# Attention and a mixture of experts in one kernel: the gate computed in each expert slot, and the order of early loads and weight splits

## The chip, the cores and the metric

The kernel runs on one core of a Trainium2 chip. Its engines each run their own queue of instructions in order: TensorE (PE in the rows; its weight loads are PEld), VectorE (DVE), ScalarE (ACT), GpSimd (POOL), and SyncE (SP), whose queue here issues most of the DMA transfers. The metric is the time of one execution on the device in microseconds; the time before is the median of three runs.

## What is computed

```python
# attention over 32 memory slots; B, H, S, D, M = 8, 8, 576, 64, 32
a = softmax(phi, axis=seq)
k_m = einsum('bhsm,bhsd->bhmd', a, k); v_m = einsum('bhsm,bhsd->bhmd', a, v)
attn = softmax(q @ k_m.T / sqrt(D)); x = (attn @ v_m)   # as (4608 tokens, 512)
# mixture of 8 experts, one for each token
logits = x @ w_gate
e_idx = argmax(logits, axis=1)
gate_w = softmax(logits)[arange(N), e_idx]
eom = 1 / (1 + exp(-(x @ w_output_gate)))
for e in range(8):
    mask = e_idx == e
    out[mask] = gate_w[mask, None] * eom[mask, e, None] * (relu(x[mask] @ w1[e]) @ w2[e])
```

## The kernel before

**Attention.** The eight batches are worked in four pairs. For each pair `memory(bp)` takes phi through an exp (`soften`), transposes it, and multiplies it with nine chunks of k and v (`sums`, L778; chunks 0 to 7 are tiles kvt, chunk 8 is kv) into k_m and v_m; `turn_kv` (L804 on TensorE, L809 and L810 on ScalarE) makes kT. The 20 turns of `attention()`, five to a pair, each take a piece of q through scores (L869), shift, exp (L889), divide, transpose and values (L916, emptied by ScalarE in L918), and store rows of x to the DRAM table xs (L1055, L1059). A row of xs is four groups of 144 numbers: 128 of x, and 16 that are that group's share of the logits of w_gate and w_output_gate.

**Order.** `ORDER` lists the steps of a turn; at each step but w, f and G the generator yields, and what was deferred (`LATE`, `hold`) comes nearer. `MEM` and `MEM0` list the steps of `memory`. Loads are issued from `loads()`, a generator that `lod.step()` moves: `NLD` steps at the start, then one in each `sums(c)` with c < 8. All issues of SP stand in one queue in the order of the program.

**Ranking.** After the fifth turn of a pair `rank(bp)` picks each token's expert, counts, and places tokens in lists (`route_early`, `route_late`, `table`). It also computes the gate of the pair's tokens (w2_, w3_, zs, gd, gt) and writes it over the 16 columns behind the first 128 of each row in xs (`gates_out`, L1008 and L1011).

**Slots.** 36 slots of three, two or one block of 128 tokens of one expert are in `order`; 14 of them run here. `gather` reads a slot's rows of xs by indirect DMA into xg, `turn_x` turns them into xh and xl (high and low parts of fp32), `Stream.split` makes high and low parts of a piece of weights (ScalarE L587, VectorE L602; eight pieces to a slot), `several` does the matmuls (L1309 or L1304 and L1305, then L1346) and `finish_y` scales by the gate and scatters. The first five slots are whole (x is transposed by TensorE, L1140); the later ones are quartered (four gathers of 144 numbers to a block, transposed by VectorE). The first slot opens in turn 17 of attention; the rest of attention and of the ranking is stepped from `hook()` inside the slots. Two pieces of weights are split in turn 16, at the two places w in ORDER; f flushes the VectorE half.

The core of it, as far as the change needs it:

```python
ORDER = ["R4", "X", "S", "G", "R0", "m", "w", "D", "G", "M", "w", "B", "f", "V0", "R1", "R1", "V1", "M", "m", "f", "W", "C"]
...
                elif w == "w":
                    if t == START - 1:
                        stream.split(2, False)
                    continue
```

Of the kernel before, what the change touches and what calls it, by code (L numbers as in the profile page):

```python
# [9 lines left out]
F32 = mybir.dt.float32  # L10
# [8 lines left out]
P = 128  # L19
# [3 lines left out]
NCH = 9  # L23
# [15 lines left out]
ORDER = ["R4", "X", "S", "G", "R0", "m", "w", "D", "G", "M", "w", "B", "f", "V0", "R1", "R1", "V1", "M", "m", "f", "W", "C"]  # L39
# [9 lines left out]
NLD = 3  # L49
# [22 lines left out]
def attention_moe(tc, phiT, kv, qT, wgo, wall, out):  # L72
# [3 lines left out]
    with contextlib.ExitStack() as ctx:  # L76
# [138 lines left out]
        def table(nm, q, nch, nblk):  # L215
# [18 lines left out]
            yield from hold(LATE["pe"])  # L234
# [498 lines left out]
        def memory(bp):  # L733
# [33 lines left out]
            def sums(c):  # L767
# [17 lines left out]
                if c < 8:  # L785
                    lod.step()
                elif b and bp + 1 < NBP:
                    load_kv(bp + 1, 8)
# [143 lines left out]
        def rank(bp, lg):  # L932

            t0 = bp * 2 * S
            lt = lg[:, :, 0:E]
            lo = lg[:, :, E:2 * E]
# [4 lines left out]
            w2_ = rt.tile(b3, F32, name="w2_")  # L941
            w3_ = rt.tile(b3, F32, name="w3_")
            pm = rt.tile([P, NCH], F32, name="pm")
            zs = rt.tile([P, NCH], F32, name="zs")
            gd = rt.tile([P, NCH], F32, name="gd")
# [4 lines left out]
            gt = rt.tile([P, NCH, XQ - P], F32, name="gt")  # L950
# [6 lines left out]
            G.tensor_tensor(w2_[:], lt, lmb, ALU.subtract)  # L957
# [8 lines left out]
            V.tensor_tensor(w3_[:], oh, lo, ALU.mult)  # L966
            A.activation(w2_[:], w2_[:], AF.Exp)
# [5 lines left out]
            V.tensor_reduce(zs[:], w3_[:], axis=AX.X, op=ALU.add)  # L973
            yield

            def rest():
# [10 lines left out]
                V.tensor_reduce(gd[:], w2_[:], axis=AX.X, op=ALU.add)  # L987
                A.activation(zs[:], zs[:], AF.Exp, scale=-1.0)
# [4 lines left out]
                V.tensor_scalar(gd[:], gd[:], 1e-9, None, ALU.add)  # L993
# [3 lines left out]
                V.tensor_scalar(zs[:], zs[:], 1.0, None, ALU.add)  # L997
# [3 lines left out]
                V.tensor_tensor(gd[:], gd[:], zs[:], ALU.mult)  # L1001
                yield
                V.tensor_copy(row[:], ri[:])  # L1003
                V.reciprocal(gd[:], gd[:])
                yield
                V.tensor_copy(gt[:], gd[:].unsqueeze(2).to_broadcast([P, NCH, XQ - P]))
                def gates_out(b):
                    nc.sync.dma_start(  # L1008
                        xs[t0 + b * S:t0 + b * S + 512, P:XQ].rearrange("(c p) d -> p c d", p=P),
                        gt[:, 4 * b:4 * b + 4])  # L1010
                    nc.sync.dma_start(xs[t0 + b * S + 512:t0 + b * S + 576, P:XQ], gt[64 * b:64 * b + 64, 8])  # L1011
# [4 lines left out]
                if bp == 1 and "open" not in env:  # L1016
                    kept.extend(functools.partial(gates_out, b) for b in range(2))
                    singly.extend(functools.partial(one_hot, c) for c in range(NCH))
                else:
                    for b in range(2):  # L1020
                        gates_out(b)
# [82 lines left out]
        def turn_x(z, c):  # L1104
# [4 lines left out]
            if c == 0:  # L1109
                z["x"] = (mo.tile([P, 4, 3 * P], F32R, name="xh"),  # L1110
                          None if nb == 2 else mo.tile([P, 4, 3 * P], F32R, name="xl"))
                if z["quart"]:
                    z["xt"] = {}
                    z["g"] = env["xt"].tile([P, 3], F32, name="gx")
                    for b in range(4):
                        k = nb - (nb == 2 and b > 1)
                        A.copy(z["g"][32 * b:32 * b + 32, 0:k], xg[0:32, 0:k, XQ * b + P])
            xh, xl = z["x"]
            if z["quart"]:
# [9 lines left out]
                if nb == 2:  # L1129
                    pt = z["xt"].pop(c)[:, 0:192]  # L1130
                    A.copy(xh[:, c, 0:192], pt)
                    V.tensor_tensor(xh[:, c, 192:384], pt, xh[:, c, 0:192].bitcast(F32), ALU.subtract)
                    return
                pt = z["xt"].pop(c)[:, 0:n]
# [8 lines left out]
            V.tensor_tensor(xl[:, c, 0:n], pt, xh[:, c, 0:n].bitcast(F32), ALU.subtract)  # L1143

# [126 lines left out]
        def finish_y(z, k, py):  # L1271
            y = mo.tile([P, DM], F32, name="y", bufs=2)
            n = P
            if (z["nb"], k) == (2, 1):

                n = 64
                ya = env["xt"].tile([64, DM], F32, name="ya", bufs=1)
                A.copy(ya[:], py[64:128])
                V.tensor_tensor(ya[:], py[0:64], ya[:], ALU.add)
                py = ya[:]  # L1280
            A.activation(y[0:n], py[0:n], AF.Copy, scale=z["g"][0:n, k:k + 1] if z["quart"] else z["xg"][:, k, P:P + 1])  # L1281
# [4 lines left out]
        def several(i, st, nxt, hook):  # L1286


            z = order[i]
            nb, x, h = z["nb"], z["x"], []  # L1290
            n_ = nb * P
            for u in range(4):
# [36 lines left out]
                hook()  # L1329
            py = [bank([DM], "ps") for _ in range(nb)]  # L1330
# [26 lines left out]
        def single(i, st, nxt):  # L1357
# [15 lines left out]
            for u in range(4):  # L1373
# [13 lines left out]
                if u < 3:  # L1387
                    st.done(PUMP[1])
            for c in range(5):
                nxt(c)  # L1390
# [36 lines left out]
        def run(st):  # L1427
# [95 lines left out]
```

## Time and profile before

| what | value |
|---|---|
| median of three runs | 551.75 us (550.49 to 555.39) |
| the profiled execution | 547.47 us |
| its span, first to last instruction | 545.8 us |
| TensorE busy | 505.4 us (93%) |
| VectorE busy | 352.2 us (65%) |
| ScalarE busy | 287.5 us (53%) |
| GpSimd busy | 238.7 us (44%) |
| mean granted clock of TensorE | 0.973 of 2.4 GHz |
| DMA | 123.54 MB, mean 226 GB/s |

The rows come from the one profiled execution, whose own time lies below all three runs; a sum of its durations stands against 547.47 us. A busy TensorE means that a matmul is in flight, and the ends of matmuls are modelled; where two follow each other, the distance of their starts is what counts. The time in front of a bracket such as [2.60 <-DMA qt<-qT] is how long the engine was idle before the row, and what ended it.

### The profile page before, as it was taken

How to read it: one execution, taken by the hardware profiler on the slowest of the kernel's cores; microseconds unless marked ns; L12 is line 12 of the kernel's file. 1: busy time of each engine (PE TensorE's matmuls, PEld its weight loads, DVE VectorE, ACT ScalarE, POOL GpSimd, SP SyncE). 2: the span in 40 equal slices, each digit the busy share in tenths (PEclk: the TensorE clock that was granted, in tenths of full speed). 3: DMA queues.
4: the chain of work that ended last, by engine and by line, in shares of the span. 5: the costliest groups of instructions: out<-in, count | busy, mean ns of one | idle time of the engine just before them, and what ended most of it. 6: DMA issues, size and time to landing. Idle time of an engine off the chain costs nothing. (4 is left out here: it accounts for less than half of the span.)

```text
span 545.8 us, 10567 instructions
## 1 busy us (share of the span) xinstructions
PE 505.4 (93%) x3850; PEld 437.8 (80%) x3850; DVE 352.2 (65%) x783; ACT 287.5 (53%) x536; POOL 238.7 (44%) x254
## 2 busy tenths in 40 slices
PE   3768688799999999999999999999999999999993
PEld 2445466598789898898998989898999899898982
DVE  4275999868865559978446546953886297639310
ACT  3465567644454365453444546853776376548310
POOL 2152568673525044320476553564447353710101
PEclk9978989989999999999999999999999999999998
DMA  8999999798767658754566574865686477743101
GB/s 282 413 410 413 410 344 368 275 367 281 205 211 237 202 199 291 223 156 131 155 189 202 178 235 134 266 217 186 212 251 198 164 249 238 236 133 98 30 20 44
DMA packets 42062, 123.54 MB, mean 226 GB/s; under 512 B 10320, under 2 KB 10384, under 8 KB 41616
## 3 DMA queue, kind: packets, MB, share of 16 engines
q1 hardware_dynamic: 35200, 102.71, 57.3%
q0 software_dynamic: 6800, 20.06, 10.4%
q8 instruction: 32, 0.52, 0.4%
q14 instruction: 30, 0.25, 0.1%
HBM read 102.40 MB, written 20.35 MB: 225 GB/s over the span
## 5 line engine op out<-in xcount | busy, mean ns | idle before, releaser
L1346 PE MATMUL bps<-whl,hh 128*128 128x512 f32 x640 | 192.3, 393 | 0.0
L1309 PE MATMUL bps<-xh,whl 128*128 128x384 f32 x640 | 166.7, 337 | 0.0
L602 DVE TENSOR_TENSOR whl<-w,whl 128x1024 fp32r<-128x1024 f32 x112 | 136.3, 1222 | 9.6 <-ACT whl L587 9.6
L1346 PEld LDWEIGHTS bps<-whl,hh 128*128 128x128 f32 x640 | 119.9, 188 | 24.5 <-issue 0.2
L587 ACT CAST whl<-w 128x1024 fp32r<-128x1024 f32 x112 | 116.1, 1044 | 13.8 <-PE bps L1346 13.7
L1309 PEld LDWEIGHTS bps<-xh,whl 128*128 128x128 f32 x640 | 116.5, 189 | 1.2 <-issue 0.6
L542 POOL DMA_INDIRECT xg<-xs,idx_ql x84 | 99.0, 1178 | 25.6 <-issue 23.5
L1309 PE MATMUL bps<-xl,whl 128*128 128x384 f32 x320 | 107.4, 336 | 0.0
L1346 PE MATMUL bps<-whl,hl 128*128 128x512 f32 x240 | 93.7, 390 | 0.0
L1314 DVE SCALAR_TENSOR_TENSOR hl<-bps,hh 128x384 fp32r<-128x384 f32 x80 | 44.0, 554 | 64.4 <-ACT hh L1313 64.4
L1313 ACT ACTIVATE hh<-bps 128x384 fp32r<-128x384 f32 x80 | 38.9, 492 | 77.0 <-PE bps L1309 73.9
L1282 POOL DMA_INDIRECT out<-y,idx_ol x23 | 25.8, 1121 | 109.7 <-ACT y L1281 54.1
L1309 PEld LDWEIGHTS bps<-xl,whl 128*128 128x128 f32 x320 | 60.5, 189 | 0.4
L1346 PEld LDWEIGHTS bps<-whl,hl 128*128 128x128 f32 x240 | 45.1, 188 | 8.5
L885 POOL TENSOR_TENSOR ea<-ea,mx 128x512 f32<-128x512 f32 (+1 forms) x20 | 19.3, 963 | 47.3 <-DVE mx L883 42.1
L1304 PE MATMUL bps<-xh,whl 128*128 128x384 f32 x128 | 37.7, 338 | 0.0
L1305 PE MATMUL bps<-xh,whl 128*128 128x256 f32 x128 | 35.7, 279 | 0.0
L1281 ACT ACTIVATE y<-bps,gx 128x512 f32<-128x512 f32 x19 | 13.1, 687 | 40.1 <-PE bps L1346 33.4
L1014 POOL TENSOR_SCALAR Aw<-iota_row,row 128x128 bf16<-128x128 bf16 x36 | 29.1, 824 | 8.4 <-DVE row L1003 8.3
L1282 POOL DMA_INDIRECT out<-y,idx_ob x9 | 10.8, 1200 | 46.6 <-ACT y L1281 37.1
L879 DVE STREAM_TRANSPOSE ea<-bpd 128x512 f32<-128x512 f32 (+1 forms) x20 | 13.2, 659 | 24.8 <-PE bpd L869 24.7
L916 PE MATMUL bpd<-ve_b,aT 64*128 64x144 f32 (+1 forms) x320 | 26.6, 314 | 2.0 <-DVE xl L1143 1.1
(277 smaller groups left out, 595.4 us busy)
## 6 DMA issues: line engine op xcount, KB each, us to landing
w<-wall SPq DMA_DIRECT2D x112, 512.0 KB, 4.4
kvt<-kv SPq DMA_DIRECT2D x32, 512.0 KB, 9.6
qt<-qT SPq DMA_DIRECT2D x16, 512.0 KB, 9.8
xs<-xo SPq DMA_DIRECT2D x8, 576.0 KB, 5.1
ph<-phiT SPq DMA_DIRECT2D x3, 1152.0 KB, 12.8
kv<-kv SPq DMA_DIRECT2D x4, 512.0 KB, 9.5
xg<-xs,idx_ql POOLq DMA_INDIRECT x84, 4.5
ph<-phiT SPq DMA_DIRECT2D x4, 288.0 KB, 4.0
```

Of the source, the lines that this page charges most:

```text
L542: G.indirect_dma_start(out=z["xg"][:, k, XQ * b:XQ * b + XQ], out_offset=None, in_=xs[0:z["rows"]].rearrange("t (a q) -> (t a) q", a=4), i ...
L587: A.copy(hl[:, 0], w[:])
L602: V.tensor_tensor(hl[:, 1], w[:], hl[:, 0].bitcast(F32), ALU.subtract)
L916: T.matmul(px[to:to + n, r, sl], z["aT"][h, o:o + n], ves[2 * bp + b][h, g], start=True, stop=True)
L1014: G.tensor_scalar(Aw[:, bp * NCH + c], iota_row[:], row[:, c:c + 1], None, ALU.is_equal)
L1282: G.indirect_dma_start(out=out, out_offset=bass.IndirectOffsetOnAxis(ap=z["idx"][1][0:n, z["q0"] + k:z["q0"] + k + 1], axis=0), in_=y[0:n] ...
L1304: T.matmul(pb, w[:, 0, o:o + P], x[0][:, cc], start=(cc == 0), stop=False)
L1305: T.matmul(pb[:, 0:256], w[:, 1, o:o + P], x[0][:, cc, 0:256], start=False, stop=(cc == 3))
L1309: T.matmul(pb, w[:, b, o:o + P], x[a][:, cc, 0:n_], start=(n == 0), stop=(n == 11))
L1313: A.activation(h_[:, j], pb, AF.Relu)
L1314: V.scalar_tensor_tensor(l_[:, j], pb, 0.0, h_[:, j].bitcast(F32), ALU.max, ALU.subtract)
L1346: T.matmul(py[k], a, w[:, b, DM * f:DM * f + DM], start=(u == 4 and f == 0 and n == 0), stop=(u == 7 and f == 1 and n == len(ps) - 1))
```

## The change

The ranking no longer computes the gate, and nothing is written over the logits in xs. Instead a new generator `gate(z)` computes it in each slot from the gathered logits: in whole slots from xg, in quartered ones from a copy `lq` that `turn_x` makes with its last chunk. `several` steps it at each hook, ahead of what the hook did before. `finish_y` takes its scale from z["g"] in all slots, and its scratch `ya` from another pool.

`NLD` goes from 3 to 2, and `sums` of pair 2's chunk 6 steps the loads twice. ORDER loses the second w, the second f and the empty place W; the second piece of weights is split after the x of slot 0. The hold before the matmuls of the table of the late lists is one step longer.

```diff
-ORDER = ["R4", "X", "S", "G", "R0", "m", "w", "D", "G", "M", "w", "B", "f", "V0", "R1", "R1", "V1", "M", "m", "f", "W", "C"]
+ORDER = ["R4", "X", "S", "G", "R0", "m", "w", "D", "G", "M", "B", "f", "V0", "R1", "R1", "V1", "M", "m", "C"]
...
-NLD = 3
+NLD = 2
...
-            yield from hold(LATE["pe"])
+            yield from hold(LATE["pe"] + (nm == "l"))
...
-                    lod.step()
+                    lod.step(2 if (bp, c) == (NBP - 2, 6) else 1)
...
         def rank(bp, lg):
...
-            G.tensor_tensor(w2_[:], lt, lmb, ALU.subtract)
...
-            V.tensor_tensor(w3_[:], oh, lo, ALU.mult)
-            A.activation(w2_[:], w2_[:], AF.Exp)
...
-            V.tensor_reduce(zs[:], w3_[:], axis=AX.X, op=ALU.add)
...
-                V.tensor_reduce(gd[:], w2_[:], axis=AX.X, op=ALU.add)
-                A.activation(zs[:], zs[:], AF.Exp, scale=-1.0)
...
-                V.tensor_scalar(gd[:], gd[:], 1e-9, None, ALU.add)
...
-                V.tensor_scalar(zs[:], zs[:], 1.0, None, ALU.add)
...
-                V.tensor_tensor(gd[:], gd[:], zs[:], ALU.mult)
...
-                V.reciprocal(gd[:], gd[:])
...
-                V.tensor_copy(gt[:], gd[:].unsqueeze(2).to_broadcast([P, NCH, XQ - P]))
-                def gates_out(b):
...
         def turn_x(z, c):
...
-                    z["g"] = env["xt"].tile([P, 3], F32, name="gx")
-                    for b in range(4):
-                        k = nb - (nb == 2 and b > 1)
-                        A.copy(z["g"][32 * b:32 * b + 32, 0:k], xg[0:32, 0:k, XQ * b + P])
...
+                if c == 3:
+                    z["lq"] = env["xt"].tile([32, 4, 12, 2 * E], F32, name="lq", bufs=1)
+                    xv = xg[:, 0:nb].rearrange("p k (b q) -> p (k b) q", b=4)[:, 0:m // 32, P:XQ]
+                    for a in range(4):
+                        A.copy(z["lq"][:, a, 0:m // 32], xv[32 * a:32 * a + 32])
...
+        def gate(z):
+
+            nb, xg, quart = z["nb"], z["xg"], z["quart"]
+            n, m = (32, 6 if nb == 2 else 4 * nb) if quart else (P, nb)
+            z["g"] = rt.tile([P, 3], F32, name="gx", bufs=2)
...
+            if quart:
+                ls, w2, w3, l3 = (z["lq"][:, a, 0:m] for a in range(4))
+                V.tensor_tensor(ls, ls, w2, ALU.add)
+                V.tensor_tensor(w3, w3, l3, ALU.add)
+                V.tensor_tensor(ls, ls, w3, ALU.add)
+                w2, w3 = w2[:, :, 0:E], w3[:, :, 0:E]
+            else:
...
+                V.tensor_reduce(ls, xg[:, 0:nb].rearrange("p k (a q) -> p k q a", a=4)[:, :, P:XQ],
+                                axis=AX.X, op=ALU.add)
+            yield
+            V.tensor_reduce(mx, ls[:, :, 0:E], axis=AX.X, op=ALU.max)
+            V.tensor_tensor(oe[:], iota_s[:, 0:E], slot[:, z["s"]:z["s"] + 1].to_broadcast([P, E]), ALU.is_equal)
+            yield
+            V.tensor_tensor(w2, ls[:, :, 0:E], mx.unsqueeze(2).to_broadcast(b3), ALU.subtract)
+            V.tensor_tensor(w3, ls[:, :, E:2 * E], oe[0:n].unsqueeze(1).to_broadcast(b3), ALU.mult)
+            yield
+            A.activation(w2, w2, AF.Exp)
+            V.tensor_reduce(zs, w3, axis=AX.X, op=ALU.add)
+            yield
+            A.activation(zs, zs, AF.Exp, scale=-1.0)
+            V.tensor_reduce(sm, w2, axis=AX.X, op=ALU.add)
+            yield
+            V.tensor_scalar(sm, sm, 1e-9, None, ALU.add)
+            V.tensor_scalar(zs, zs, 1.0, None, ALU.add)
+            V.tensor_tensor(g, sm, zs, ALU.mult)
+            if not quart:
+                V.reciprocal(z["g"][:, 0:nb], g)
+                return
+            V.reciprocal(g, g)
+            yield
+            for b in range(4):
+                k = nb - (nb == 2 and b > 1)
+                A.copy(z["g"][32 * b:32 * b + 32, 0:k], g[:, b:4 * k - 3 + b:4])
...
-            A.activation(y[0:n], py[0:n], AF.Copy, scale=z["g"][0:n, k:k + 1] if z["quart"] else z["xg"][:, k, P:P + 1])
+            A.activation(y[0:n], py[0:n], AF.Copy, scale=z["g"][0:n, k:k + 1])
...
-        def several(i, st, nxt, hook):
+        def several(i, st, nxt, hook_):
...
+            gen = gate(z)
+
+            def hook():
+                next(gen, None)
+                hook_()
...
                 if i == lo:
                     for c in range(5):
                         turn_x(order[i], c)
+                    if not lo:
+                        st.split(2)
```

The loads, on the SP queue, from the second piece of phi (ph) on; kvt and kv are chunks of k and v, qt pieces of q, xs<-xo the first store of x. Before:

```order
L674 DMA ph<-phiT 128x2304
L684 DMA qt<-qT 128x1024
L689 DMA kvt<-kv 128x1024 x2
L684 DMA qt<-qT 128x1024
L674 DMA ph<-phiT 128x2304
L689 DMA kv_391<-kv 128x1024
L689 DMA kvt<-kv 128x1024 x4
L684 DMA qt<-qT 128x512
L684 DMA qt<-qT 128x1024 x2
L1055 DMA xs<-xo 128x2x576
L689 DMA kvt<-kv 128x1024 x4
```

And now, on the same queue from the same place:

```order
L674 DMA ph<-phiT 128x2304
L684 DMA qt<-qT 128x1024 x2
L674 DMA ph<-phiT 128x2304
L689 DMA kv_387<-kv 128x1024
L689 DMA kvt<-kv 128x1024 x4
L684 DMA qt<-qT 128x512
L684 DMA qt<-qT 128x1024 x2
L1029 DMA xs<-xo 128x2x576
L689 DMA kvt<-kv 128x1024 x4
```

Six chunks of pair 1 stood ahead of the short piece of q (qt 128x512, the one of turn 4); now four do, and the other two come behind the store.

The opening of the first slot on ScalarE: whl<-w is the high half of a split, xo the emptied values, xh the x of the slot, hh its first results. Before:

```order
L810 COPY vT_b<-bpa 64x256
L587 CAST whl<-w 128x1024 x2
L918 COPY xo<-bpd 128x576 x2
L889 ACTIVATE ea_207<-ea_207 128x16x32
L1142 CAST xh<-bps 128x384 x4
L1313 ACTIVATE hh<-bps 128x384 x2
```

And now on ScalarE at the same place:

```order
L810 COPY vT_b<-bpa 64x256
L587 CAST whl<-w 128x1024
L918 COPY xo<-bpd 128x576 x2
L889 ACTIVATE ea_207<-ea_207 128x16x32
L1117 CAST xh<-bps 128x384 x4
L587 CAST whl<-w 128x1024
L1340 ACTIVATE hh<-bps 128x384 x2
```

The second split stood ahead of the copies of the values and now stands behind the x of the slot.

VectorE from the x of slot 0 (xl) on; hl frees the PSUM bank of a first result, ea, mx, lg and sa are attention. Before:

```order
L1143 TENSOR_TENSOR xl<-bps,xh 128x384 x4
L1314 SCALAR_TENSOR_TENSOR hl<-bps,hh 128x384
L879 STREAM_TRANSPOSE ea_208<-bpd 128x16x32
L883 TENSOR_REDUCE mx<-ea_208 128x16
L1072 TENSOR_REDUCE lg<-xo 128x32
L1314 SCALAR_TENSOR_TENSOR hl<-bps,hh 128x384
L602 TENSOR_TENSOR whl<-w,whl 128x1024 x2
L895 TENSOR_REDUCE sa<-ea_207 128x16
```

And now on VectorE, with the first steps of the gate (gl, gs, oe):

```order
L1118 TENSOR_TENSOR xl<-bps,xh 128x384 x4
L602 TENSOR_TENSOR whl<-w,whl 128x1024
L1341 SCALAR_TENSOR_TENSOR hl<-bps,hh 128x384
L1139 TENSOR_REDUCE gl<-xg 128x48
L879 STREAM_TRANSPOSE ea_208<-bpd 128x16x32
L883 TENSOR_REDUCE mx<-ea_208 128x16
L1046 TENSOR_REDUCE lg<-xo 128x32
L1341 SCALAR_TENSOR_TENSOR hl<-bps,hh 128x384
L602 TENSOR_TENSOR whl<-w,whl 128x1024 x2
L1142 TENSOR_REDUCE gs<-gl 128x3
L1143 TENSOR_TENSOR oe<-iota_s,slot 128x8
L895 TENSOR_REDUCE sa<-ea_207 128x16
```

A step of the gate comes behind each hl, ahead of attention's steps, and the second split's VectorE half stands in front of the first hl.

## Rows read from the trace of the kernel before

**Rows 1.** Windows: stretch, its length, each engine's busy us (instructions), granted clock, DMA share, GB/s.

```profile
57.00:79.00 22.00, 16.64 (x314) 11.67 (x306) 21.09 (x80) 12.61 (x30) 13.68 (x21) 0.92 1.02 381
...
105.00:115.00 10.00, 7.74 (x62) 6.27 (x61) 6.51 (x12) 5.62 (x11) 8.91 (x9) 0.66 0.68 232
115.00:156.00 41.00, 39.58 (x293) 33.10 (x292) 34.81 (x90) 20.35 (x34) 20.01 (x23) 1.00 0.83 266
...
229.00:537.00 308.00, 307.86 (x1642) 280.69 (x1640) 186.44 (x319) 161.78 (x294) 132.77 (x114) 1.00 0.57 175
```

**Rows 2.** Timeline of TensorE, 38 to 50 us: start, us, line, tiles, count, [idle before <-releaser].

```profile
38.36 1.08 PE L778 MATMUL pk<-kvt,at 128*32 128x128 f32 x32
42.04 0.54 PE L869 MATMUL bpd<-qt,kT 64*32 64x64 f32 x32 [2.60 <-DMA qt<-qT]
...
46.92 1.08 PE L778 MATMUL pk<-kvt,at 128*32 128x128 f32 x32
...
49.00 0.94 PE L869 MATMUL bpd<-qt,kT 64*32 64x256 f32 x16 [0.63 <-ACT kT L809]
```

**Rows 3.** Timeline of the SP queue: start and length of the issue.

```profile
30.85 4.39 SPq L684 DMA_DIRECT2D qt<-qT  x3
...
71.18 0.33 SPq L684 DMA_DIRECT2D qt<-qT  x1
...
73.23 0.56 SPq L1011 DMA_DIRECT2D xs<-gt  x1
...
95.06 0.41 SPq L684 DMA_DIRECT2D qt<-qT  x1
```

**Rows 4.** DMA view, 28 to 42 us: all packets together.

```profile
DMA packets 1490, 5.71 MB, mean 408 GB/s; under 512 B 159, under 2 KB 159, under 8 KB 1360
```

**Rows 5.** DMA view of single issues (30.85, 71.18, 73.23, 95.06): KB, us to landing.

```profile
qt<-qT SPq DMA_DIRECT2D x1, 256.0 KB, 11.1
...
qt<-qT SPq DMA_DIRECT2D x1, 512.0 KB, 5.8
...
xs<-gt SPq DMA_DIRECT2D x1, 4.0 KB, 4.7
...
qt<-qT SPq DMA_DIRECT2D x1, 512.0 KB, 9.8
```

**Rows 6.** Timeline of VectorE in the ranking of pair 0, 62 to 70 us.

```profile
62.84 0.23 DVE L966 TENSOR_TENSOR w__959<-ohg,lg 128x72 f32<-128x72 bf16 x1
62.98 0.17 DVE L972 CAST ohc<-oc 128x8 bf16<-128x8 f32 x1
...
69.46 0.30 DVE L1006 COPY gt<-gd 128x144 f32<-128x144 f32 x1
69.67 0.16 DVE L186 TENSOR_REDUCE cs<-cle 128x2 f32<-128x16 f32 x1
```

**Rows 7.** Timelines of TensorE and ScalarE, 67 to 75 us.

```profile
67.67 0.19 PE L981 MATMUL pr<-ohg,strict 128*128 128x72 bf16 x1 [2.10 <-DVE tge L194]
...
74.64 0.78 ACT L725 ACTIVATE ph<-ph,nmx 128x576 f32<-128x576 f32 x1 [0.53 <-DVE nmx L721]
```

**Rows 8.** Timeline of ScalarE ahead of the first slot.

```profile
105.03 1.99 ACT L587 CAST whl<-w 128x1024 fp32r<-128x1024 f32 x2
107.04 1.18 ACT L918 COPY xo<-bpd 128x576 f32<-128x576 f32 x2
```

**Rows 9.** Timeline of TensorE into the first slot.

```profile
107.73 1.11 PE L869 MATMUL bpd<-qt,kT 64*32 64x256 f32 x16 [2.26 <-ACT xo L918]
108.78 2.97 PE L1140 MATMUL bps<-ident,xg 128*128 128x128 f32 x12
111.48 0.69 PE L1309 MATMUL bps<-xh,whl 128*128 128x384 f32 x1
...
114.10 0.51 PE L1309 MATMUL bps<-xh,whl 128*128 128x384 f32 x2
114.45 0.33 PE L1309 MATMUL bps<-xl,whl 128*128 128x384 f32 x1
```

More of the change, by code (lines that the diff above doesn't have):

```diff
@@ L932, in rank @@
         def rank(bp, lg):
-            t0 = bp * 2 * S
             lt = lg[:, :, 0:E]
-            lo = lg[:, :, E:2 * E]
             b3 = [P, NCH, E]
@@ L949, in rank @@
             row = rt.tile([P, NCH], F32, name="row", bufs=2)
-            gt = rt.tile([P, NCH, XQ - P], F32, name="gt")
             oh = ohg[:, cs]
@@ L1016, in rest @@
                 if bp == 1 and "open" not in env:
-                    kept.extend(functools.partial(gates_out, b) for b in range(2))
                     singly.extend(functools.partial(one_hot, c) for c in range(NCH))
                 else:
-                    for b in range(2):
-                        gates_out(b)
                     for c in range(NCH):
@@ L1128, in turn_x @@
                     return
[L1129 to L1134, printed above, removed]
+                m = 192 if nb == 2 else n
+                pt = z["xt"].pop(c)[:, 0:m]
+                A.copy(xh[:, c, 0:m], pt)
+                V.tensor_tensor(xh[:, c, 192:384] if nb == 2 else xl[:, c, 0:n], pt, xh[:, c, 0:m].bitcast(F32),
+                                ALU.subtract)
+                if c == 3:
[4 more added lines that the diff above has]
+                return
             else:
@@ L1143, in turn_x @@
             V.tensor_tensor(xl[:, c, 0:n], pt, xh[:, c, 0:n].bitcast(F32), ALU.subtract)
+        def gate(z):
+            nb, xg, quart = z["nb"], z["xg"], z["quart"]
+            n, m = (32, 6 if nb == 2 else 4 * nb) if quart else (P, nb)
+            z["g"] = rt.tile([P, 3], F32, name="gx", bufs=2)
+            tl, mm = (env["xt"], 12) if quart else (rt, 3)
+            sm_ = tl.tile([n, 4, mm], F32, name="gs", bufs=1)
+            mx, sm, zs, g = (sm_[:, i, 0:m] for i in range(4))
+            oe = rt.tile([P, E], F32, name="oe")
+            b3 = [n, m, E]
+            if quart:
[5 more added lines that the diff above has]
+            else:
+                ls, w2, w3 = (rt.tile([P, mm, w], F32, name=nm)[:, 0:m]
+                              for nm, w in (("gl", 2 * E), ("gw", E), ("go", E)))
+                V.tensor_reduce(ls, xg[:, 0:nb].rearrange("p k (a q) -> p k q a", a=4)[:, :, P:XQ],
[18 more added lines that the diff above has]
+                V.reciprocal(z["g"][:, 0:nb], g)
+                return
+            V.reciprocal(g, g)
[3 more added lines that the diff above has]
+                A.copy(z["g"][32 * b:32 * b + 32, 0:k], g[:, b:4 * k - 3 + b:4])
@@ L1276, in finish_y @@
                 n = 64
[L1277 to L1280, printed above, removed]
-            A.activation(y[0:n], py[0:n], AF.Copy, scale=z["g"][0:n, k:k + 1] if z["quart"] else z["xg"][:, k, P:P + 1])
+                ya = env["hs"].tile([P, F], F32, name="hs")[0:64, 0:DM]
+                A.copy(ya, py[64:128])
+                V.tensor_tensor(ya, py[0:64], ya, ALU.add)
+                py = ya
+            A.activation(y[0:n], py[0:n], AF.Copy, scale=z["g"][0:n, k:k + 1])
             G.indirect_dma_start(
@@ L1329, in several @@
                 hook()
+            last(gen)
             py = [bank([DM], "ps") for _ in range(nb)]
@@ L1388, in single @@
                     st.done(PUMP[1])
+            last(gate(z))
             for c in range(5):
```

8 lines of the change are left out of this document (removed).

## The prediction

> **What bounds the kernel now.** I read the windows first, to see where TensorE is not busy. From 229 to 537 us it is busy for 307.86 of 308 us at full clock, and from 115 to 156 us for 39.58 of 41 us [rows 1]: there the time is a fixed sum of matmuls, and only a new wait could change it. The change does not touch those matmuls. What is left is the stretch before the first slot, whose first expert matmul starts at 111.48 us [rows 9], and I followed the waits back from there. Three parts of it set that start.
>
> First, the loads. Between 28 and 42 us the DMA engines move 408 GB/s without a pause [rows 4], so the SP queue is a line in which each piece lands after the bytes ahead of it. At 38.36 us TensorE has all but run out of work, and at 42.04 us the scores of turn 4 (L869) begin 2.60 us late, on a piece of q [rows 2]. That piece was issued at 30.85 us [rows 3] and took 11.1 us to land [rows 5]: it was not issued late, it stood behind other loads.
>
> Second, VectorE, which is busy for 21.09 of 22 us from 57 to 79 us [rows 1]. Both the ranking of pair 0 and the attention turns pass through it there; TensorE waits 2.10 us at 67.67 us for it (L981) [rows 7].
>
> Third, the last microseconds. ScalarE splits two pieces of weights at 105.03 us and only then, at 107.04 us, empties the banks of the values (L918) [rows 8]; the scores of turn 17 wait 2.26 us for that, and the transposes of x and the first expert matmul follow them in TensorE's order [rows 9].
>
> **Part 1, k and v later (NLD 2).** Two chunks of k and v, 512 KB each, move from ahead of q's piece of turn 4 to behind the first store of x; so do all later ones by one step, until pair 2's chunk 6 steps twice and the old lead is back. A chunk is 524,288 bytes, at 408 GB/s 1.29 us, so q lands at 30.85 + 11.1 - 2 x 1.29 = 39.4 us, and 2.5 us of the wait at 42.04 go. What is late next is the two chunks themselves (L778 at 46.92 us, 32 matmuls, the second half on the second chunk). Behind q's piece now come two pieces of q, the store (576 KB, 1.45 us) and then they: 39.4 + 2 x 1.29 + 1.45 + 2 x 1.29 = 46.0 us for the second. Its half began at 46.92 + 1.08 / 2 = 47.46, so from there on 1.5 us are won. The transposes behind it (L804) and the copy of kT that ends the wait at 49.00 [rows 2] then have a ScalarE that is 2.5 us earlier in front of them, so a little more survives: between 1.5 and 1.9, and I take 1.7 us. The bounds are 2.5 (the chunks come in time) and 0 (the chunks come as late as q did); a loss needs the second chunk to land after 47.46, for which the line would have to stand still for 1.5 us.
>
> **Part 2, gates out of the ranking.** Eight small VectorE instructions of each ranking go (L966, L973, L987, L993, L997, L1001, L1004, L1006), with two on ScalarE, one on GpSimd and four writes of 64-byte rows on SP. Of the four rankings the first lies in the saturated stretch. Counted from start to start, the first of its eight costs 62.98 - 62.84 = 0.14 us and the last 69.67 - 69.46 = 0.21 us [rows 6]; the eight together 1.0 us. Not all of it reaches TensorE. Two of them (0.29 us) stand ahead of the instruction that L981 waits for; the other six lie behind it, and pay through the exp of phi at 74.64 us, which waits 0.53 us for VectorE and has the copy of kT behind it [rows 7]. So 0.3 to 1.0 us; I take 0.7. The second ranking lies at 89 to 99 us, where TensorE goes from instruction to instruction, and the last two beside the slots: 0.
>
> The four writes of pair 0 hold up the line too. The piece of q ahead of them was issued at 71.18 us [rows 3] and landed 5.8 us later, the last write at 73.23 and 4.7 [rows 5]: (73.23 + 4.7) - (71.18 + 5.8) = 0.95 us. This is no term of the sum, since TensorE does not wait for loads there, but it sets a limit: the q of turn 17, issued at 95.06 us and landed 9.8 us later, at 104.86, can now come at 103.9, and the scores at 107.73 cannot gain more than about 3.7 us.
>
> **Part 3, the second split.** The two splits take 1.99 us [rows 8]; one moves behind the x casts of slot 0. The copy of the values and the scores of turn 17 come 1.0 us earlier (0 if q is late after all). The moved split costs nothing there: piece 1 is wanted by matmul 25 of the slot, about 5 us after its start, and ScalarE and VectorE idle there (the window from 105 to 115 us has them busy 5.62 and 6.51 of 10 us [rows 1]). Its load of the next raw piece is issued later as well; that piece is for the fifth part of the slot, some 20 us on.
>
> **Part 4, gates in the slots.** Each slot gets 11 to 13 small VectorE instructions and 2 (whole slots) or 6 (quartered ones: two Exp and four copies of the logits) more on ScalarE. Per whole slot: a reduction of 192 elements, for which L1006 of 0.30 us is the nearest shown row, and ten near 0.2 us or below [rows 6]: at most 2.1 us, and about 1.2 us by the spacing from start to start. They are queued ahead of the next step of attention and behind the instruction that frees the PSUM bank (L1314), and TensorE works from banks and split weights made earlier. In the stretch from 115 to 156 us VectorE has 41 - 34.81 = 6 us to spare [rows 1], from which rank 2's eight leave too; from 229 us on it is busy 186 of 308 us. I take 0, with 2.1 us a slot as the upper bound.
>
> [...]
>
> **Also moved.** The empty place W and three weight places leave ORDER: a turn of attention has 15 steps instead of 16, so attention ends some two hooks earlier in slot 1. The gathers of the late slots stand one output earlier on GpSimd, in spite of the longer hold. Neither has a wait to shorten.
>
> **Sum.** 1.7 + 0.7 + 1.0 = 3.4 us, below the limit of 3.7. The profiled execution took 547.47 us (span 545.8), so 544.1; the runs' median of 551.75 lies 4.3 us above it, and I take the gain from the median: **548.3 us**. Its own range, from the bounds (0 + 0.3 + 0 to 3.7) and 1 us of slots, is 546.5 to 551.
>
> **Rivals.**
> *The clock stays full.* From 105 to 115 us the granted clock is 0.66 on average [rows 1], that is, mostly the 1.2 GHz level, and it fell after the wait of 2.26 us. The wait shrinks to 1.3. Should the clock now hold at 2.4 GHz, then the first eight matmuls come every 0.175 us (114.45 - 114.10, two of them) and not in 2.62 us (111.48 to 114.10): 1.2 us; the transposes about 1.9 in place of 2.70 us (an estimate: at the full rate 1.35, plus what the casts hold them up), and the scores 0.66 for 1.11 [rows 9]: 2.4 us in all, 545.9 us. For it: the stretch from 115 to 156 us, with 1.4 us of waits spread over it, stands at 1.00 [rows 1], and the wait shrinks by nearly half. Against it: from 57 to 79 us, with its wait of 2.10 us, the clock stands at 0.92, so it fell there too [rows 1, 7], and 1.3 us is still the longest wait of the opening's end. Chance 0.22.
> *k and v starve TensorE.* The stores of x wait for ScalarE, and the chunks now stand behind them. If the second chunk comes 1.5 us later than I sum, part 1 is gone: 551.75 - 1.7 = 550.0 us. For it: the margin is small, and the line is full to 105 us. Against: the same bytes stand ahead of the chunk after them as before. Chance 0.24.
> *The slots pay for the gates: slower.* Before attention ends the slots have three banks, and L1314 waits behind whatever VectorE was given at the last hook. If each of the five whole slots pays its 2.1 us in full, 10.5 - 3.4 = 7.1 us are lost: 558.9 us. It decides from 3.4 us of TensorE waits behind the bank-freeing instruction or the split weights. Against: after 115 us the trace shows about 1.4 us of idle TensorE before 156 and almost none later. Chance 0.07.
>
> **How the numbers follow.** The forecast has 0.47, the rivals 0.22, 0.24 and 0.07. Range 544.5 to 551.3 us: it holds the clock's case with about 1 us below, and the starved one with about 1 above, and leaves out the slower one and the tails. A change within 1% (546.2 to 557.3 us) can hardly be told from none by this measurement, whose runs spread over 550.49 to 555.39. Faster by over 1%: most of the clock's case and the lower tail of the forecast, 0.27; slower by over 1%: 0.06; the rest 0.67.
>
> **What would show it.** Right: the scores of turn 4 begin near 39.5 us, those of turn 5 near 47.3, turn 17 near 104.3 us after about 1.3 us of wait for the copy of the values, and the first expert matmul near 108; from there to the last matmul as long as before, 425 us. Part 1 is wrong if the L778 of chunk 4 waits for loads beyond 46 us; part 2 if VectorE's stretch shrinks by less than 0.9 us or TensorE then waits for ScalarE instead; part 3 if turn 17 waits for q. Part 4 is wrong if any wait of TensorE after 115 us names VectorE for more than a microsecond. The whole is wrong if the sum of matmuls itself takes longer.

## The result, and the profile after

The changed kernel takes 556.58 us (median of 22 runs, 553.27 to 564.08) where the kernel before takes 551.75 (22 runs): ratio 1.0104, 95% interval 1.0076 to 1.0131, 5.7 us slower. Ratios and their intervals leave out the runs that lie over 1.5% above the fastest of their kernel, while the medians are over all runs, so that the two can differ a little. The forecast of 548.3 us was wrong, and so was its sign. The profiled execution took 553.73 us, span 551.9.

I read the opening first. TensorE's timeline (start, us, line, tiles, count) shows what parts 1 and 3 foresaw:

```profile
40.46 0.46 PE L869 MATMUL bpd<-qt,kT 64*32 64x64 f32 x32
...
45.44 0.65 PE L778 MATMUL pk<-kvt,at 128*32 128x128 f32 x16 [0.61 <-DMA kvt<-kv]
46.80 0.94 PE L869 MATMUL bpd<-qt,kT 64*32 64x256 f32 x16 [0.35 <-ACT kT L809]
...
106.06 0.67 PE L869 MATMUL bpd<-qt,kT 64*32 64x256 f32 x16 [1.32 <-ACT xo L918]
...
108.83 0.44 PE L1336 MATMUL bps<-xh,whl 128*128 128x384 f32 x1
```

The wait for q is gone, turn 5 begins 2.2 us earlier [rows 2], the wait for the values fell from 2.26 to 1.32 us, and the first expert matmul comes 2.65 us earlier [rows 9]. Turn 17 itself came only 1.67 us earlier, at 106.06 us where the prediction had 104.3; the other 0.98 us were won behind it, where the granted clock stayed at 1.00 (second row below). From the first expert matmul to TensorE's last instruction at 543.28 us, however, it takes 434.4 us where the forecast had 425. The windows (length, then busy us and instructions of TensorE, its weight loads, VectorE, ScalarE, GpSimd; granted clock, DMA share, GB/s) place the loss in the stretch that was to stay as it was:

```profile
57.00:79.00 22.00, 16.77 (x304) 11.52 (x296) 19.28 (x68) 10.61 (x23) 11.94 (x18) 0.84 1.00 390
104.00:114.00 10.00, 8.17 (x84) 7.13 (x81) 8.54 (x17) 6.87 (x13) 8.66 (x9) 1.00 0.85 298
...
229.00:537.00 308.00, 303.23 (x1604) 273.11 (x1602) 202.92 (x444) 173.96 (x349) 130.50 (x113) 1.00 0.57 172
```

TensorE was busy for 307.86 of these 308 us [rows 1]. Its waits after 112 us (us in total, times, longest):

```profile
PE bps L1336 <- DVE xl L1102: 3.8, 7, 0.8
PE bpd L1115 <- DMA xg<-xs,idx_gb: 1.3, 2, 1.1
...
PE bps L1374 <- issue: 0.3, 1, 0.3
```

The first two did not exist before, when the waits of the same stretch were these:

```profile
PE bpd L916 <- DVE xl L1143: 1.1, 1, 1.1
PE bpd L1140 <- ACT xo L918: 0.3, 1, 0.3
```

The view counts idle time alone, and the matmuls next to a wait follow each other more slowly too (0.28 us from 348.95 to 349.23 and from 350.55 to 350.83, behind the two waits of slot 7, in place of 0.17 from 347.25 to 347.42), so the loss is read from starts. To see which slots pay, I took for each slot the start of its first matmul (x times the first weights), of its second half (L1374, before L1346: the second weights) and of the next slot, in us:

| trace | first expert matmul | slot 0 | slot 1 | first halves of 7, 9, 11, 13 |
|---|---|---|---|---|
| before | 111.48 | 44.32 | 37.66 | 16.67, 16.67, 16.67, 16.67 |
| before, second trace | 111.65 | 43.21 | 37.65 | 16.67, 16.67, 16.67, 16.67 |
| after | 108.83 | 43.05 | 39.52 | 18.32, 18.61, 18.61, 18.19 |
| after, second trace | 106.50 | 43.05 | 39.43 | 18.32, 18.34, 19.00, 18.20 |
| opening edits alone | 107.15 | 42.49 | 39.47 | 16.67 each |
| gates in slots alone | 110.40 | 43.21 | 37.63 | 18.33, 18.45, 18.62, 18.29 |
| no gate in slots of two | 111.51 | 43.09 | 39.45 | 16.67 each |
| no gate in quartered slots of three | 106.43 | 43.05 | 38.80 | 18.24, 18.29, 18.67, 18.16 |
| gate computed a slot ahead | 110.62 | 43.05 | 39.67 | 16.67 each |
| W kept | 108.19 | 43.21 | 37.61 | 18.33, 18.56, 18.75, 18.32 |
| k and v alone | 111.36 | 44.14 | 37.63 | 16.67 each |
| split alone | 108.66 | 43.21 | 37.65 | 16.67 each |
| a slot ahead, W kept | 110.01 | 43.20 | 37.63 | 16.67 each |
| late copies | 110.28 | 43.04 | 40.01 | 17.32, 17.27, 17.81, 17.10 |

Slots 6, 8, 10 and 12 have two blocks, 7, 9, 11 and 13 are the slots of three behind them. These four lose 1.65 + 1.94 + 1.94 + 1.52 = 7.05 us in their first halves, slot 1 loses 1.9; slots 2 to 6 stay within 0.2 us. In this trace the second halves of slots 9 and 11 are 0.7 and 0.6 us longer as well, which the second trace does not repeat.

How a slot of two makes the next one late is read from slot 6 (from 328.79 us) on VectorE of the changed kernel; gs holds the gate's small sums, gx the finished scale:

```profile
340.74 0.18 DVE L1160 RECIPROCAL gs<-gs 32x6 f32<-32x6 f32 x1
340.85 0.30 DVE L1344 TENSOR_TENSOR hl<-bps,hl 128x192 f32<-128x192 f32 x1
342.12 0.36 DVE L1344 TENSOR_TENSOR hl<-bps,hl 128x192 f32<-128x192 f32 x1 [0.97 <-ACT hl L1343]
...
349.94 0.55 DVE L1102 TENSOR_TENSOR xl<-xt,xh 128x384 fp32r<-128x384 f32 x1
```

and on its ScalarE:

```profile
340.95 0.80 ACT L1164 COPY gx<-gs 32x2 f32<-32x2 f32 x4 [0.73 <-DVE gs L1160]
341.77 0.32 ACT L1343 COPY hl<-bps 128x192 f32<-128x192 f32 x1
```

ScalarE waits 0.73 us for the gate's last step and copies for 0.8; the copy of a result (L1343) stands behind that, and VectorE idles 0.97 us for it. All that VectorE has queued, weights and the next x among it, moves back, so that the last piece of x of slot 7 is ready at 350.49, 3.2 us after the slot's start (347.25). Before, it was ready 0.55 us after the start of slot 7 at 349.24:

```profile
349.24 0.55 DVE L1143 TENSOR_TENSOR xl<-xt,xh 128x384 fp32r<-128x384 f32 x1
```

TensorE of the changed kernel stops for it:

```profile
348.95 0.44 PE L1336 MATMUL bps<-xl,whl 128*128 128x384 f32 x1 [0.26 <-DVE xl L1102]
...
350.55 0.45 PE L1336 MATMUL bps<-xl,whl 128*128 128x384 f32 x1 [0.74 <-DVE xl L1102]
```

ScalarE took its queue in order here: L1343 starts at 341.77, behind the copies, though VectorE had been idle for it since 341.15.

That the slots of two had no room stood in the trace of before, in a window I had not cut, from 330.78 to 349.24 us:

```profile
330.78:349.24 18.46, 18.46 (x106) 16.89 (x105) 16.20 (x31) 14.29 (x29) 10.30 (x8) 1.00 0.74 226
```

VectorE is busy for 16.20 of 18.46 us and passes results to and fro with ScalarE (14.29 us); slot 5, of three blocks, has 16.27 us of VectorE in 33.03. The stretch on which the prediction rested has 186 of 308 us [rows 1], a mean over slots of two and of three.

### The profile page after: what moved, and what is told of

It is laid out like the page before. It is cut to its first block, busy times and chain, and to the rows that moved or that the text cites. A ratio compares the mean times of both kernels' runs of the same rounds, so it can differ in the third digit from the quotient of the medians.

```text
span 551.9 us, 10711 instructions
## 1 busy us (share of the span) xinstructions
PE 508.7 (92%) x3850; PEld 435.3 (79%) x3850; DVE 373.9 (68%) x923; ACT 301.8 (55%) x592; POOL 238.1 (43%) x250
## 5 line engine op out<-in xcount | busy, mean ns | idle before, releaser
L1374 PE MATMUL bps<-whl,hh 128*128 128x512 f32 x640 | 192.4, 393 | 0.0
L1374 PEld LDWEIGHTS bps<-whl,hh 128*128 128x128 f32 x640 | 120.0, 188 | 24.9 <-issue 0.7
L542 POOL DMA_INDIRECT xg<-xs,idx_ql x84 | 100.6, 1197 | 25.6 <-issue 23.8
L1374 PE MATMUL bps<-whl,hl 128*128 128x512 f32 x240 | 93.8, 391 | 0.7 <-DVE xt L1094 0.4
L1374 PEld LDWEIGHTS bps<-whl,hl 128*128 128x128 f32 x240 | 45.1, 188 | 9.5 <-issue 1.0
L1302 ACT ACTIVATE y<-bps,gx 128x512 f32<-128x512 f32 x34 | 23.4, 688 | 51.0 <-PE bps L1374 30.5
L1303 POOL DMA_INDIRECT out<-y,idx_ob x9 | 9.1, 1012 | 52.9 <-ACT y L1302 41.1
L1102 DVE TENSOR_TENSOR xh<-xt,xh 128x192 fp32r<-128x192 f32 x16 | 5.7, 357 | 34.0 <-ACT xh L1101 19.9
```

The source lines that it names most:

```text
L542: G.indirect_dma_start(out=z["xg"][:, k, XQ * b:XQ * b + XQ], out_offset=None, in_=xs[0:z["rows"]].rearrange("t (a q) -> (t a) q", a=4), i ...
L1303: G.indirect_dma_start(out=out, out_offset=bass.IndirectOffsetOnAxis(ap=z["idx"][1][0:n, z["q0"] + k:z["q0"] + k + 1], axis=0), in_=y[0:n] ...
L1374: T.matmul(py[k], a, w[:, b, DM * f:DM * f + DM], start=(u == 4 and f == 0 and n == 0), stop=(u == 7 and f == 1 and n == len(ps) - 1))
```

## The experiments

Each experiment is compared with runs of the kernel before that were taken beside it; their median lies between 545.27 and 551.35 us.

**Which half of the change loses.** The change was cut in two: the kernel before with the opening edits, and the changed kernel with the opening of before.

The first is before with these lines; the second is after without them:

```diff
-NLD = 3
+NLD = 2
...
-                    lod.step()
+                    lod.step(2 if (bp, c) == (NBP - 2, 6) else 1)
...
+                    if not lo:
+                        st.split(2)
```

ORDER and the hold go with them.

> The kernel before with the opening edits alone (NLD 2 and its double step, the shorter ORDER, the second split behind the x of slot 0, the longer hold); the gate stays in the ranking. Theory A (the opening gains, the gates in the slots lose): the first expert matmul comes about 2 us earlier than the 111.48 us of before, the slots take their 425.4 us as before, so 551.75 - 2 = 549.7 us, ratio 0.996. Theory B (the loss after the opening belongs to the earlier opening itself: gathers, rankings and weights that come late for slots which now start sooner): the slots take some 9 us longer, about 558 us, ratio 1.012.

> The changed kernel with the opening edits undone: gates in the slots alone. Theory A: the first expert matmul at about 110.8 us (the eight instructions of the ranking of pair 0 are gone, 0.7 us), the slots some 9 us longer, so 551.75 - 0.7 + 9 = 560 us, ratio 1.015. Theory B: the slots as before, 551 us, ratio 0.999.

The opening alone: 550.38 against 550.42 us, ratio 1.0033 (0.9993 to 1.0074). The four x waits are absent, so theory A has the gates right; but slot 1 takes 39.47 us, so B is right about slot 1. A's time (0.996) did not come: slots 4, 7 and 9 of its trace are 6.0 us longer, behind stalls that are taken up further down. The gates alone (four runs): 1.0164 (1.0089 to 1.024), all four waits there, slot 1 at 37.63 us as before. The loss has two sources, one in each half.

**Which gate work.** Two kernels leave out the gate of one kind of slot; the second has 3 for the 2.

```diff
+            if quart and nb == 2:
+                z["g"] = g1
+                return
...
-                if c == 3:
+                if c == 3 and nb != 2:
```

> The changed kernel, but slots of two blocks compute no gate: their scale is a constant one (this part of the output is left out). Their gate steps and the four copies of gx go, and the four copies of their logits, which stand in the slot ahead. Theory A1 (VectorE and ScalarE have no room in a slot of two blocks, whose weights and next x pass through them, and the gate steps there make the x of the next slot of three late): the slots behind them take 33.03 us again instead of 34.7 to 35.7, so 8.5 us of 556.6 go, 548.1 us, ratio to before 0.993. Theory A2 (it is the four copies of the logits of the next slot, 1.44 us of ScalarE at the end of the slot of two blocks, which stay here): 556 us, ratio 1.008. Theory C (the scratch ya in another pool, or the other order of gathers and scatters): 556 us too.

> The changed kernel, but quartered slots of three blocks compute no gate: their scale is a constant one (this part of the output is left out). That takes the four copies of their logits (1.44 us of ScalarE) out of the slot of two blocks ahead, where the steps of that slot's own gate stay. Theory A1: the late x is still late, since VectorE's and ScalarE's gate steps stand ahead of it; the slots behind slots of two still take about 34.5 us, 1 us or less is won, 555.6 to 556.6 us, ratio 1.007 to 1.010. Theory A2: those slots take 33.03 us again, 548.1 us, ratio 0.993.

Without gates in slots of two: ratio 1.000 (0.9964 to 1.0037), the slots behind them back at 16.67 us. Without those in slots of three (four runs): 1.0129 (1.0073 to 1.0185), the waits stay, with 6.69 us in place of 7.05. The gate of the slot of two is the cause (A1); the logit copies hardly matter, the pool of `ya` not at all. VectorE's window over slot 6 of the first of these kernels reads like that of before:

```profile
334.75:353.21 18.46, 18.46 (x106) 16.89 (x104) 16.16 (x32) 13.59 (x26) 9.73 (x8) 1.00 0.75 229
```

**The same work elsewhere; the place W; two opening edits by themselves.**

```diff
+                if step == 2 and nb == 3 and 8 * i + 8 < st.hi and order[i + 1]["nb"] == 2:
+                    gen[0] = gate(order[i + 1])
...
-ORDER = [..., "M", "m", "C"]
+ORDER = [..., "M", "m", "W", "C"]
```

> The changed kernel with the same gate work in other places: a slot of two blocks has its gate computed in the second half of the slot of three ahead of it, and a quartered slot of three copies its logits at its own first hook, no longer at the end of the slot of two. Nothing is left out. Theory A1 (no room in slots of two): the slots behind them take 33.03 us again and nothing else gets longer, so about 7 us of 556.6 go, 549.5 us, ratio to before about 1.00, as with the bare slots of two (1.000). Rival (the gate costs VectorE and ScalarE the same wherever it stands, and is paid in the slots of three instead): 555 to 557 us, ratio 1.01.

> The changed kernel with the empty place W back in ORDER, so that a turn of attention has 16 steps again as before. Theory W (the shorter turn moves attention against the hooks, and the lists from which slot 2 is gathered come 1.2 us later in slot 1): the wait of the transposes in slot 1 for the gathered rows goes, slot 1 takes about 37.7 us in place of 39.5, so 556.6 - 1.8 = 554.8 us. Rival (the other opening edits, above all the longer hold, make the gathers late): slot 1 stays at 39.5 us, 556.6 us.

> The kernel before with NLD 2 and the double step alone. By the prediction's part 1 the scores of turn 4 lose their wait of 2.60 us and those of turn 5 come 1.7 us earlier; the rest of the opening follows, first expert matmul near 109.8 us, 550.0 us, ratio 0.997. Rival (what is won there is lost in the saturated stretch from 57 to 79 us, where VectorE has no room): first expert matmul at 111.5 us, 551.7 us.

> The kernel before with the second split moved behind the x of slot 0, alone (W stays, so a turn keeps its 16 steps). By the prediction's part 3 the scores of turn 17 come 1.0 us earlier, their wait for the copy of the values is 1.3 us, the first expert matmul comes near 110.5 us, 550.7 us. If the clock then holds at 2.4 GHz, another 2.4 us: near 108.9 us for the first expert matmul or its equal within slot 0, 548.4 us. If the second split in slot 0 delays it instead: slot 0 longer than its 44.3 us by 1 us or more, 551.7 us.

Computing the same gates a slot ahead removes all four waits: 549.51 against 551.35 us, ratio 0.9925 (0.9882 to 0.9968). So the price is one of place, not of work: in the last but one run below, which has the same gates a slot ahead, the slots of three stand at 33.03 and 33.19 us, as before. With W kept, slot 1 falls to 37.61 us (ratio 1.0117, 1.001 to 1.0224, of few runs and with the gates still in the slots of two). The list that slot 2's gathers wait for comes later without W. In the changed kernel (slot 1 from 151.88) on VectorE, GpSimd and TensorE:

```profile
165.60 0.17 DVE L254 SCALAR_TENSOR_TENSOR idx_ob<-iv,i 128x9 int32<-128x9 f32 x1
...
165.77 1.06 POOL L548 DMA_INDIRECT xg<-xs,idx_gb  x1 [4.76 <-DVE idx_ob L254]
...
176.33 0.33 PE L1115 MATMUL bpd<-ident,xg 128*128 128x128 f32 x1 [1.07 <-DMA xg<-xs,idx_gb]
```

and with W (slot 1 from 151.40):

```profile
164.02 0.17 DVE L254 SCALAR_TENSOR_TENSOR idx_ob<-iv,i 128x9 int32<-128x9 f32 x1
...
173.88 0.49 PE L1115 MATMUL bpd<-ident,xg 128*128 128x128 f32 x3
```

13.7 us into the slot against 12.6, and no wait. k and v alone: 550.48 us, ratio 0.9997 (0.9958 to 1.0035). Its scores of turns 4 to 6 are

```profile
38.98 0.45 PE L869 MATMUL bpd<-qt,kT 64*32 64x64 f32 x32
47.08 1.38 PE L869 MATMUL bpd<-qt,kT 64*32 64x256 f32 x16 [0.35 <-ACT kT L809]
53.18 0.66 PE L869 MATMUL bpd<-qt,kT 64*32 64x256 f32 x16
```

and its window from 45 to 55 us

```profile
45.00:55.00 10.00, 9.12 (x135) 5.66 (x137) 3.90 (x9) 4.44 (x12) 1.62 (x2) 0.66 1.02 383
```

Turn 5 is 1.9 us early (1.7 foreseen), but in this trace the granted clock is 0.66 from 45 to 55 us, where it was 0.97 before, and by turn 6 (53.18, before 53.09) the gain is gone. The split alone: 0.9988 (0.9937 to 1.0039), the last wait 1.32 us, slot 0 not longer, the first expert matmul at 108.66. That is the time foreseen for a clock that holds (108.9), not for the wait alone (110.5), and the clock did hold; the second row is the second trace of before:

```profile
105.00:115.00 10.00, 8.60 (x64) 7.67 (x64) 8.19 (x16) 6.91 (x13) 9.20 (x10) 1.00 0.79 271
...
105.00:115.00 10.00, 7.65 (x71) 6.08 (x68) 6.99 (x13) 6.25 (x11) 8.75 (x9) 0.83 0.69 239
```

**The losses put right together; the copies alone; both kernels traced again.** The first has both remedies. In the second the four gx copies of a slot of two come eight steps later, behind the casts of the next x.

```diff
             V.reciprocal(g, g)
-            yield
+            for _ in range(8 if nb == 2 else 1):
+                yield
```

> The changed kernel with the gates of slots of two computed in the slot of three ahead (as in the run with the gate work in other places) and W kept in ORDER. If the losses of the change are these two and they add, slots 1, 7, 9, 11 and 13 stand at 37.6 and 33.0 to 33.2 us, 7.3 + 1.8 = 9.1 us of 556.6 go, 547.5 us, ratio to before 0.992. Rival (with the shorter turn gone, what it gave to slot 0 and to attention is gone too): 549.5 us as without W.

> The changed kernel, but in slots of two the four copies of gx (ScalarE, behind VectorE's reciprocal) stand behind the last x cast of the next slot instead of between two copies of results; VectorE's gate steps stay where they were. Theory S (it is ScalarE's wait for VectorE's last gate step, and the 0.8 us of copies behind it, that hold up the results and so VectorE): 1.5 of the 1.7 us a slot go, slots 7, 9, 11 and 13 at 33.0 to 33.6 us, 550.5 us, ratio 1.000. Theory V (it is the time of VectorE's own steps): the slots stay at 34.5 us and above, 556 us, ratio 1.010. In between, each has its share.

> The kernel before, traced once more. If stalls of TensorE that nothing releases (0.3 to 1.7 us, behind a run of gathers) come by chance, this trace has some where the first had none, and the slots add up to up to 5 us more than 425.4 us; if they belong to the changed programs, there are none again. The first expert matmul within 2 us of 111.48, by the stretches of the opening at half clock.

> The changed kernel, traced once more. The waits for the x of slots 7, 9, 11 and 13 (1.65 us each or more) and that for the gathered rows in slot 1 (1.3 us) are there again; stalls that nothing releases stand elsewhere if they come by chance. The first expert matmul between 106 and 112 us, by the stretches of the opening at half clock.

Both remedies: 545.76 us against 549.37, ratio 0.9938 (0.9907 to 0.9969), that is 3.4 us (1.7 to 5.1) under the kernel before. Late copies: 1.0011 (0.998 to 1.0041); the first halves exceed 16.67 by 2.82 us in all, not 7.05. So 60% of the loss was ScalarE's wait for VectorE and its copies. The 0.7 us a slot that are left go with the rest of the gate, VectorE's 13 steps, ScalarE's two Exp and the copies in their new place, which were not taken apart; neither theory holds alone. The second trace of before (552.85 us) has what the first lacked, stalls that nothing in the profile releases (`<-issue`); on TensorE and GpSimd:

```profile
426.92 0.40 PE L1346 MATMUL bps<-whl,hh 128*128 128x512 f32 x1 [1.04 <-issue]
...
427.65 0.49 PE L1346 MATMUL bps<-whl,hh 128*128 128x512 f32 x1 [0.33 <-issue]
...
425.35 1.09 POOL L542 DMA_INDIRECT xg<-xs,idx_ql  x1 [0.30 <-issue]
```

The GpSimd row is the last of a run of 12 gathers. The slots hit (7, 9, 11) are 1.0, 3.8 and 1.4 us longer. Behind the longest stall of all traces, 1.72 us in that with the opening edits, the clock fell too: the granted clock is 0.60 from 374 to 376 us and 0.54 from 376 to 378. The second trace of after has the same waits for x and no stall.

**Do the gathers cause those stalls?** In the best kernel and in that of before, fills of a small tile were put between the quartered gathers: first four behind each gather, then one behind every second.

```diff
+                        if b % 2:
+                            G.memset(env["fill"][:], 0.0)
```

> The kernel of the run with gates computed ahead and W kept, with four idle fills of a small tile on GpSimd behind each quartered gather, so that a run of 12 takes some 21 us in place of 15 to 16. Theory P (TensorE's stalls without a releaser belong to runs of 12 gathers at full pace: in the traces so far nearly all of them stand behind runs whose first and last start are 14.5 to 15.5 us apart): no such stall in this trace, slots 5, 7, 9 and 11 at 33.03 us, and some 2 us less than the 545.8 us of that kernel, ratio to before 0.990. Rival (the stalls come behind any run of gathers, or by other chance): stalls again, ratio 0.994.

> The kernel before with the same idle fills behind its quartered gathers, nothing else. Theory P: no stalls without a releaser in its trace; the second trace of the kernel before had 6 us of them, the first none, so some 3 us less in the median, ratio 0.995, and less spread between runs. Rival: as before, ratio 1.000, or slower where the fills make the gathered rows late.

> As the best kernel, with one short fill of a small tile on GpSimd behind every second quartered gather, in place of four behind each, which had made the gathers themselves the bound (2.45 us each). By the rows of that run a fill adds some 0.45 us, so a run of 12 takes about 17.7 us and the rows still come in time. Theory P (TensorE's stalls without a releaser belong to runs at full pace): none in this trace, slots 5, 7, 9 and 11 near 33.03 us, ratio to before 0.990. Rival (they come behind any run of gathers): stalls again in one or two slots, ratio 0.994; if the gathers are late again, slots of two get longer.

> The kernel before with one short fill behind every second quartered gather, nothing else. Theory P: no stalls without a releaser, the median some 3 us below that of before, ratio 0.995. Rival: as before, ratio 1.000.

Four fills were a failed size, 612.33 and 615.35 us (1.1193 and 1.1227): GpSimd became the bound, the scatter of y came late, and with it the buffer of the next y, the bank and the next slot. In the kernel with both remedies, called the best kernel here:

```profile
PE bps L1333 <- ACT y L1304: 36.0, 4, 10.3
```

One fill: no stall in either trace. In the best kernel the first and last start of a run of 12 lie 17.1 to 18.7 us apart with it; in that of before 15.4 to 16.8, hardly more than the 15.7 to 16.0 of its first trace, which had no fill and no stall either, so this second trace says little. The best kernel takes 543.81 us (12 runs, 542.66 to 544.71), ratio 0.9966 (0.9943 to 0.9989); before with fills 545.28 against 545.27, ratio 1.0007 (0.9975 to 1.0039). A gain in time from the fills is not shown: the best kernel was not run without them in that round, where the kernel before itself took 545.27 us and may have had few stalls to lose.

## Why the prediction was wrong

*Part 4 failed*, at the step "I take 0". It priced the gate's steps by VectorE's spare time in the mean, named the five whole slots as the place, and had TensorE work "from banks and split weights made earlier", which leaves out the next slot's x. The whole slots pay nothing: with W kept, slots 0 and 1 stand at 43.21 and 37.61 us, as in the second trace of before. The slots of two pay, through the next slot's x: 7.05 us, shown by taking their gate out, by moving it a slot ahead, and in part by moving the copies. The rival "the slots pay" had the sign and nearly the size (7.1 us net foreseen), with the wrong place and only part of the mechanism: it priced VectorE's rows alone, and 60% was ScalarE standing behind a step of VectorE. That a slot of two costs 1.5 to 2.3 us in the two traces, close to the bound of 2.1, is therefore luck. The sign set for part 4 (a wait that names VectorE for more than a microsecond) never came in a single wait: the longest is 0.8 us, and the loss came from seven of them.

What the steps take on VectorE is not what reaches TensorE: in slot 6 the durations of the 13 VectorE steps of the gate sum to 2.6 us, and TensorE loses 0.7 us a slot with the copies out of the way.

*"Also moved" failed too*: "Neither has a wait to shorten" holds, but dropping W made a new one, 1.8 to 1.9 us in slot 1. It had been read as a matter of order alone; a step of attention more or less per turn also moves the ranking against the gathers.

*Parts 1 and 3 held in kind.* The scores of turn 4 came 1.6 us earlier (2.5 foreseen), turn 5 came 2.2 us earlier (1.7 foreseen, the second chunk waited for with 0.61 us, within the margin feared by the second rival); the wait for the values fell by 0.94 us (1.0 foreseen) in every trace with the moved split. *Part 2* is not resolved: from 57 to 79 us VectorE's busy time fell by 1.81 us between the first traces, by 0.64 between the second ones (0.9 was set as its sign), and with the gates alone it rose by 0.09; the clock differs from trace to trace there too (0.92, 0.84).

*The sum* of 3.4 us can be read over traces only. The first expert matmul came at 106.43 to 111.51 us in eleven traces with the opening edits (mean 108.85; four of them keep W, one keeps the gates in the ranking) and at 110.40 to 114.01 in five with the old opening (mean 112.27; one has the gates out of the ranking): 3.4 us. The spread of each group is as large, and 0.7 of the 3.4 is the clock's, which the sum left out: up to turn 17 the means differ by 2.75 us. That the two agree is luck.

*The clock's rival* (chance 0.22) came true at the end of the opening, where the forecast did not have it. The levels that it calls 1.2 and 2.4 GHz are the granted clocks of 0.50 and 1.00: in the first trace of before the clock is 0.50 from 108 to 113 us, and matmuls of 384 columns start every 0.32 us (112.28 to 112.92, two of them), 1.2 columns a nanosecond; behind that, at 1.00, every 0.175 us [rows 9]. From the scores of turn 17 to the first expert matmul it takes 2.77 us at a granted clock of 1.00 in all twelve traces with the shorter wait of 1.3 us. In the six with the wait of 2.26 us the clock is 0.50 to 0.76 and the stretch 2.86 to 3.75 us in five, and 1.00 and 2.77 us in one (the kernel before with one fill). So the shorter wait goes with the full clock, and the one exception shows that the longer wait does not always bring it down. The rest of that rival, the first matmuls of slot 0, does not need the change: its first half takes 19.74 us in the second trace of before too (first trace 20.85).

Together: +7.05 + 1.8 - 3.4 = 5.45 us, where the runs have 5.7 (4.2 to 7.2). The run with both losses put right agrees, 3.4 us (1.7 to 5.1) under before. The opening alone does not: by this account it should gain 1.6 us, and it took 1.8 us more (-0.4 to 4.1); the 6.0 us of stalls in its trace may be why, which is not shown. The gap of 4.3 us between the profile and the median, which the forecast carried along unnamed, fits the stalls: the first trace of before had none, its second (552.85 us) some 6 us. Two of the prediction's figures do not follow from its own terms, without bearing on this: 107.73 - 103.9 gives a limit of 3.8, not 3.7, and its bounds with 1 us of slots give 547.05 to 552.45, not 546.5 to 551.

## What to carry to other kernels

Cut the windows by the unit of work that repeats, each kind of slot by itself, before calling an engine idle: 186 of 308 us hid 16.2 of 18.5 in every second slot from slot 6 on. Before adding small steps to two engines that pass results to and fro, ask what stands behind the step that waits for the other engine, and let the sign of failure be the sum of the waits, not the longest; the same work may be free one slot earlier. A place in a hand-made order that looks empty can be what keeps two streams in step.

## What the runs showed of the hardware that was not expected

TensorE stops for 0.1 to 1.7 us at a time with nothing in the profile to release it, behind runs of indirect gathers on GpSimd. Over the 16 traces without the four fills there are 77 runs of exactly 12 gathers. Where the first and last start were less than 15.45 us apart (a limit drawn afterwards, from these same traces), 20 of 22 were followed by such a stall within 4 us; where further, 2 of 55 (0.31 us, and 0.44 us that the trace puts down to VectorE). The short runs of 6 had none beyond the waits for x. What passes between the two engines was not found, nor whether something third slows TensorE where the gathers run at full pace. That the gathers cause the stalls rests on this count, not on the fills.

The granted clock of TensorE fell around the wait of 2.26 us ahead of turn 17 in five of six traces (0.50 to 0.76 behind it), and stood at 1.00 behind the wait of 1.3 us in twelve of twelve.
